# Attention products with V issued four items after a unit's scores instead of three

## Chip, cores and metric

The kernel runs on one core of one Trainium2 chip. The metric is the device time of one execution in microseconds (us). Engines are named as the profile names them: PE is TensorE's matmul stream and PEld its weight loads, DVE is VectorE, ACT is ScalarE, POOL is GpSimd, SP is SyncE, which issues the DMAs here.

## What is computed

Chunked attention with memory keys, then two feed-forward layers. In short:

```python
# attention: batch 4, heads 8, sequence 768, head size 64, chunks of 32 queries
for c in range(24):
    k_full = concat([mem_k, k[l_start:r_end]])      # 8 memory rows and up to 56 rows around the chunk
    a = softmax(scale * q_c @ k_full.T)
    out[c] = a @ v_full
x = out.transpose(0, 2, 1, 3).reshape(3072, 512)
h = x @ w_in                                        # 512 -> 2048
x = np.maximum(0.01 * h, h) @ w_out                 # 2048 -> 512
return (x @ w_a) * (x @ w_b) @ w_out2               # 512 -> 1536 -> 512
```

## The kernel before

**Attention units.** The 3072 tokens are cut into 24 units of 128 tokens. Four units make one block of 512 tokens, the width of a matmul in the layers behind. For each unit six steps run: `a_scores` (L193, 32 small matmuls of q and k into the PSUM tile `s`), `a_soft1` (L212, on DVE the maximum L215 and the subtraction L217, on ACT the exponential L220), `a_soft2` (L223, sum, reciprocal and scaling on DVE, L230 to L233), `a_turn` (L237, sixteen 32x32 DVE transposes L246 into the tile `pt`), `a_pv` (L266, 32 small matmuls L276 of `pt` and `v` into the PSUM tile `pv`), and `a_out` (L286), which splits `pv` into a rounded part `xh` by an ACT copy (L289) and a remainder `xl` by a DVE subtraction (L290). `xh` and `xl` of a block are what the first layer reads. `load_v` (L437) issues the two V loads (L189) of the unit after next on SP; their buffers are those that `a_pv` has just read.

**First layer.** The loop over `items` (L590) runs the first feed-forward layer block by block. Block 0 has 19 items and block 1 to 5 have 16 each; an item is one slice `f` of 128 hidden features. In an item `mm1` (L377) multiplies x with a slice of w_in: 12 matmuls (L303 reads `xh`, L304 reads `xl`, L305 reads `xh`). ACT and DVE make the activation `g` from the PSUM tile `h` (L383, L385) and split it into `gh` and `gl` (L320, L321; L321 runs on POOL in block 0, on DVE later). `mm2` (L388) multiplies the `g` of the item two before with w_out: 12 matmuls (L400, L403, L404) into the four PSUM tiles `a` of the block. After a block's last `mm2` ACT and DVE copy these four tiles out (L414, L412); the next block's `mm2` writes the same four tiles. In block 0 the two halves of 256 tokens run shifted by three items, so that its items have two 256-wide parts.

**What stands beside the items.** The dictionary `beside` (L428) lists for an item the attention steps of the next block's units; they are issued right after the item's `mm1` and `mm2` (L609). For a unit whose scores stand at item f, the steps stood at f (scores, loads of q and k, first softmax part), f+1 (second part), f+2 (transposes), f+3 (products with V, V loads, copies to x). The next unit's scores stand at f+3 as well, behind those products. In block 0 the scores stand at items 5, 8, 11, 14, in blocks 1 to 4 at 2, 5, 8, 11.

**Weights.** In block 0 the first layer's weights are made from raw 64-bit words: DVE joins them (L83, L86, L87), ACT rounds (L93), POOL subtracts (L94). In blocks 1 to 4 `prep_steps` (L476) does the same for the third and fourth layer's weights, in a ring of raw load (L473), ACT scaling (L79), DVE joins and sums (L83 to L87, L490 to L493), ACT rounding, POOL subtraction and a store (L507, L517), with one buffer for each stage. The weights of `mm2` come back from memory by the loads `w<-wod` (L586).

**What sets the order.** Each engine runs its own instructions in the order in which they stand in its queue. The queues are not written out by hand: a scheduler makes them when the kernel is built, from the program order and from when it reckons an operand to be ready, so that on DVE, ACT and SP steps of neighbouring items are mixed. On PE the order is that of the program except where operands were reckoned late.

Of the kernel before, what the change touches and what calls it, by code (L numbers as in the profile page):

```python
# [18 lines left out]
UT = 128  # L19
# [5 lines left out]
NF1, NF2 = F1 // P, F2 // P  # L25
# [6 lines left out]
def kernel(  # L32
# [30 lines left out]
    ps_h, ps_s, ps_a = [p.__enter__() for p in psum1]  # L63
# [353 lines left out]
    HALF, LEAD = TB // 2, 3  # L417
# [12 lines left out]
    def at(bi, f, fn, *args):  # L430
        beside.setdefault((bi, f), []).append(lambda: fn(*args))
# [19 lines left out]
    at(0, 1, a_out, 3, ("x", 0), 3 * UT)  # L451
    at(0, 1, load_v, 3)
    at(0, 1, load_qk, 3)
    for bi in range(NB3 - 1):
        for k, f in enumerate([5, 8, 11, 14] if bi == 0 else [2, 5, 8, 11]):
            u = (bi + 1) * (TB // UT) + k
            at(bi, f, a_scores, u)
            at(bi, f, load_qk, u)
            at(bi, f, a_soft1, u)
            at(bi, f + 1, a_soft2, u)  # L460
            at(bi, f + 2, a_turn, u)
            at(bi, f + 3, a_pv, u, ps_s, "s")
            at(bi, f + 3, load_v, u)
            at(bi, f + 3, a_out, u, ("x", bi + 1), k * UT)

# [277 lines left out]
    later = []  # L745
# [87 lines left out]
```

## Time and profile before

| | us |
|---|---|
| median of 3 runs | 1226.71 (1224.39 to 1227.79) |
| the profiled execution | 1226.21 |
| its span in the trace | 1224.4 |
| PE busy | 1170.7 |
| DVE busy | 752.9 |
| ACT busy | 383.1 |
| POOL busy | 145.4 |

The profile has a page with the busy time of each engine, and the trace behind it can be asked for the waits of an engine, for a timeline of its instructions and for busy times by stage. In a timeline a row gives start, duration, engine, line, operation, output and inputs, and in square brackets the idle time of the engine before the instruction with the instruction that ended it. A waiting matmul shows the idle time of PE, not of the whole kernel.

### The profile page before, as it was taken

The numbers are of one execution on the slowest core, as the hardware profiler recorded it, in microseconds if no ns is written. First come the engines' busy times: TensorE is split into PE (matmuls) and PEld (weight loads), VectorE is DVE, ScalarE is ACT, GpSimd is POOL, SyncE is SP. The second block draws the span as 40 slices with busy tenths as digits, with TensorE's granted clock in tenths as the row PEclk, the third lists the DMA queues.
The fourth block names the chain that finished last, engine by engine and source line by source line (L and its number), as shares of the span: only waits on it lengthen the run. The fifth ranks groups of instructions, "written<-read, shape, count | busy, mean of one in ns | idle before, by whom it ended". The sixth has DMA issues, their size and how long they took to land.

```text
span 1224.4 us, 16825 instructions
## 1 busy us (share of the span) xinstructions
PE 1170.7 (96%) x6632; PEld 984.1 (80%) x6632; DVE 752.9 (61%) x1313; ACT 383.1 (31%) x642; POOL 145.4 (12%) x109
## 2 busy tenths in 40 slices
PE   5788799989998999999999999999999999999998
PEld 5778788867887887888888888888888888888887
DVE  5999959795897899666622443447443447433443
ACT  3634333243334433222422222224122223222220
POOL 1544512032122222000000000000000000000000
PEclk9898999989999999999999999999999999999999
DMA  9766658768887887642633843537453535453512
GB/s 322 256 229 194 210 186 306 268 238 299 297 304 254 310 311 261 212 138 86 221 106 108 319 158 120 193 125 280 162 215 130 198 131 208 158 204 120 189 61 103
DMA packets 63822, 250.72 MB, mean 205 GB/s; under 512 B 7424, under 2 KB 8832, under 8 KB 56832
## 3 DMA queue, kind: packets, MB, share of 16 engines
q1 hardware_dynamic: 63744, 249.66, 57.5%
q8 instruction: 52, 0.85, 0.3%
q14 instruction: 26, 0.21, 0.1%
HBM read 200.34 MB, written 49.28 MB: 204 GB/s over the span
## 4 chain that ended last, share of the span: by engine, by line
PE 67%; DVE 2%; DMA 1%; issue 0%; POOL 0%; SPq 0%; DVEq 0%; POOLq 0%
PE o L729 5%; PE o L730 5%; PE o L731 5%; PE A L662 4%; PE A L663 4%; PE A L664 4%; PE h L303 4%; PE a L403 4%; PE a L404 4%; PE a L400 4%; PE h L304 3%; PE h L305 3%; PE C L662 3%; PE C L663 3%; PE C L664 3%; PE D L663 1%
## 5 line engine op out<-in xcount | busy, mean ns | idle before, releaser
L303 PE MATMUL h<-xh,w 128*128 128x512 f32 (+1 forms) x448 | 168.8, 377 | 17.5 <-POOL w L94 14.7
L400 PE MATMUL a<-gh,w 128*128 128x512 f32 (+1 forms) x448 | 161.3, 360 | 4.8 <-DVE x L412 2.3
L304 PE MATMUL h<-xl,w 128*128 128x512 f32 (+1 forms) x448 | 164.2, 367 | 0.5 <-DVE xl L290 0.5
L305 PE MATMUL h<-xh,w 128*128 128x512 f32 (+1 forms) x448 | 163.7, 365 | 0.0
L403 PE MATMUL a<-gl,w 128*128 128x512 f32 (+1 forms) x448 | 160.8, 359 | 0.0
L404 PE MATMUL a<-gh,w 128*128 128x512 f32 (+1 forms) x448 | 160.8, 359 | 0.0
L303 PEld LDWEIGHTS h<-xh,w 128*128 128x128 f32 x448 | 87.5, 195 | 33.2 <-POOL w L94 15.7
L729 PE MATMUL o<-w,cl 128*128 128x512 f32 x288 | 112.1, 389 | 0.2 <-DMA w<-wod 0.2
L730 PE MATMUL o<-w,ch 128*128 128x512 f32 x288 | 112.0, 389 | 0.0
L731 PE MATMUL o<-w,ch 128*128 128x512 f32 x288 | 112.0, 389 | 0.0
L385 DVE TENSOR_TENSOR g<-t,h 128x512 f32<-128x512 f32 (+1 forms) x99 | 66.1, 668 | 67.3 <-ACT t L383 66.5
L320 ACT CAST gh<-g 128x512 fp32r<-128x512 f32 (+1 forms) x99 | 60.1, 607 | 149.5 <-DVE g L385 144.1
L246 DVE STREAM_TRANSPOSE pt<-p 32x128 f32<-32x128 f32 x320 | 96.8, 302 | 5.5
L400 PEld LDWEIGHTS a<-gh,w 128*128 128x128 f32 x448 | 84.6, 189 | 18.6 <-DVE x L412 2.9
L304 PEld LDWEIGHTS h<-xl,w 128*128 128x128 f32 x448 | 87.7, 196 | 13.1 <-DVE xl L290 0.9
L305 PEld LDWEIGHTS h<-xh,w 128*128 128x128 f32 x448 | 87.0, 194 | 13.3
L404 PEld LDWEIGHTS a<-gh,w 128*128 128x128 f32 x448 | 84.7, 189 | 12.5
L403 PEld LDWEIGHTS a<-gl,w 128*128 128x128 f32 x448 | 84.6, 189 | 12.5
L383 ACT ACTIVATE t<-h 128x512 f32<-128x512 f32 (+1 forms) x99 | 57.5, 581 | 110.3 <-PE h L305 110.3
L684 DVE TENSOR_TENSOR ga<-u,C 128x512 f32<-128x512 f32 x36 | 24.8, 688 | 105.4 <-ACT u L676 76.2
L676 ACT COPY u<-A 128x512 f32<-128x512 f32 x72 | 42.3, 587 | 143.5 <-PE A L664 143.5
L662 PE MATMUL A<-ch,wab 128*128 128x512 f32 x216 | 84.1, 389 | 0.0
(95 smaller groups left out, 2116.3 us busy)
## 6 DMA issues: line engine op xcount, KB each, us to landing
wab<-wab SPq DMA_DIRECT2D x36, 1792.0 KB, 7.3
w<-wod SPq DMA_DIRECT2D x116, 512.0 KB, 4.7
raw<-w SPq DMA_DIRECT2D x68, 512.0 KB, 5.9
wab<-pw SPq DMA_DIRECT2D x12, 1792.0 KB, 6.7
k<-kl SPq DMA_DIRECT2D x48, 256.0 KB, 4.3
v<-vl SPq DMA_DIRECT2D x48, 256.0 KB, 4.7
wod<-w SPq DMA_DIRECT2D x16, 512.0 KB, 5.3
q<-ql SPq DMA_DIRECT2D x48, 128.0 KB, 4.1
```

Source lines behind the costliest of these rows:

```text
L246: nc.vector.transpose(out=pt[o0:o0 + 32, :, 2 * cpar + hpar, hpx, :], in_=p[i0:i0 + 32, hpx::2, 32 * b:32 * b + 32],)
L303: nc.tensor.matmul(ps, w[1], x[0], start=first, stop=False)
L304: nc.tensor.matmul(ps, w[0], x[1], start=False, stop=False)
L305: nc.tensor.matmul(ps, w[0], x[0], start=False, stop=last)
L400: nc.tensor.matmul(ps, slot[:, 1, c], gh[:, t], start=f == 0 and o == 0, stop=False, **kw)
L403: nc.tensor.matmul(ps, slot[:, 0, c], gl[:, t], start=False, stop=False, **kw)
L404: nc.tensor.matmul(ps, slot[:, 0, c], gh[:, t], start=False, stop=f == NF1 - 1, **kw)
L662: nc.tensor.matmul(ps, w[:, 1, i, c], hi[:, kc], start=first and kc == 0, stop=False, **kw)
L663: nc.tensor.matmul(ps, w[:, 0, i, c], lo[:, kc], start=False, stop=False, **kw)
L729: nc.tensor.matmul(o, cl[:, q], w[:, 0, :], start=k == 0, stop=False)
L730: nc.tensor.matmul(o, ch[:, q], w[:, 1, :], start=False, stop=False)
L731: nc.tensor.matmul(o, ch[:, q], w[:, 0, :], start=False, stop=k == NCH - 1)
```

## The change

For the units of blocks 1 to 5 (u = 4 to 23) the three steps `a_pv`, `load_v` and `a_out` are put at f+4 instead of f+3, if that item still exists in the block; otherwise they stay at f+3. With scores at 5, 8, 11, 14 of 19 items, and at 2, 5, 8, 11 of 16 items, f+4 is at most 18 and at most 15, so that all 20 units move.

```diff
+    def last_item(bi):
+        return NF1 + LEAD if bi == 0 else NF1
+
     for bi in range(NB3 - 1):
         for k, f in enumerate([5, 8, 11, 14] if bi == 0 else [2, 5, 8, 11]):
             u = (bi + 1) * (TB // UT) + k
             at(bi, f, a_scores, u)
             at(bi, f, load_qk, u)
             at(bi, f, a_soft1, u)
             at(bi, f + 1, a_soft2, u)
             at(bi, f + 2, a_turn, u)
-            at(bi, f + 3, a_pv, u, ps_s, "s")
-            at(bi, f + 3, load_v, u)
-            at(bi, f + 3, a_out, u, ("x", bi + 1), k * UT)
+            later = (bi, f + 4) if f + 4 < last_item(bi) else (bi, f + 3)
+            at(*later, a_pv, u, ps_s, "s")
+            at(*later, load_v, u)
+            at(*later, a_out, u, ("x", bi + 1), k * UT)
```

## Rows read from the trace of the kernel before

**Rows 1.** The page's first part: busy time, share of the span and instructions of each engine.

```profile
PE 1170.7 (96%) x6632; PEld 984.1 (80%) x6632; DVE 752.9 (61%) x1313; ACT 383.1 (31%) x642; POOL 145.4 (12%) x109
```

**Rows 2.** The waits of PE: who waited for whom, total us, how many times, the longest.

```profile
PE pv L276 <- DVE pt L246: 18.5, 16, 2.7
PE h L303 <- POOL w L94: 14.7, 6, 5.8
```

**Rows 3.** Busy time by stretch: the second half of block 0, the end of block 1, and most of block 3. Columns: stretch, its length, busy us (instructions) of PE, PEld, DVE, ACT and POOL, granted clock, DMA share, GB/s.

```profile
84.00:168.00 84.00, 68.43 (x637) 65.42 (x636) 73.92 (x136) 32.77 (x60) 36.39 (x27) 0.88 0.57 188
244.00:278.00 34.00, 29.07 (x169) 23.52 (x165) 30.77 (x59) 14.12 (x25) 10.00 (x6) 0.90 0.69 251
388.00:470.00 82.00, 82.00 (x537) 68.32 (x536) 70.34 (x143) 33.59 (x56) 18.10 (x13) 1.00 0.87 302
```

**Rows 4.** Timeline of PE: the first matmul of `mm1` in items of blocks 3 to 5 that run without a stall. The first pair has a V product and scores between its items, the second pair scores alone, the third a V product alone; the item after the last pair has neither.

```profile
537.49 0.39 PE L303 MATMUL h<-xh,w 128*128 128x512 f32 x1
...
551.48 0.39 PE L303 MATMUL h<-xh,w 128*128 128x512 f32 x1
...
499.59 0.39 PE L303 MATMUL h<-xh,w 128*128 128x512 f32 x1
...
512.63 0.39 PE L303 MATMUL h<-xh,w 128*128 128x512 f32 x1
...
576.35 0.39 PE L303 MATMUL h<-xh,w 128*128 128x512 f32 x1
...
588.53 0.39 PE L303 MATMUL h<-xh,w 128*128 128x512 f32 x1
...
593.97 0.39 PE L303 MATMUL h<-xh,w 128*128 128x512 f32 x1
```

**Rows 5.** Timelines of PE and DVE in block 0: `mm1` of item 14, the copy of unit 6 to x and the first softmax step of unit 7 on DVE, and the `mm2` of block 0 that waits for a copy out of its PSUM tiles.

```profile
132.61 0.35 PE L303 MATMUL h<-xh,w 128*128 128x256 f32 x1 [1.19 <-DVE g L385]
...
151.50 0.69 DVE L290 TENSOR_TENSOR xl<-pv,xh 128x512 fp32r<-128x512 f32 x1 [1.75 <-ACT xh L289]
152.11 0.68 DVE L215 TENSOR_REDUCE m<-s 128x8 f32<-128x512 f32 x1
...
163.12 0.39 PE L400 MATMUL a<-gh,w 128*128 128x256 f32 x1 [1.97 <-ACT x L414]
```

**Rows 6.** Timelines of PE, ACT and DVE at the end of block 1 and the start of block 2: `mm1` of item 14, the longest stop inside a V product (unit 11), the first `mm1` of block 2, and the stop of its first `mm2`.

```profile
257.73 0.50 PE L303 MATMUL h<-xh,w 128*128 128x512 f32 x1 [0.66 <-DVE g L385]
...
267.52 0.47 PE L276 MATMUL pv<-pt,v 128*64 128x64 f32 x2 [2.71 <-DVE pt L246]
...
277.50 0.39 PE L303 MATMUL h<-xh,w 128*128 128x512 f32 x1
...
293.79 0.65 ACT L79 ACTIVATE raw<-raw 128x512 f32<-128x512 f32 x1 [1.71 <-DMA raw<-w]
...
294.47 0.43 DVE L83 TENSOR_SCALAR pz<-raw 128x512 int32<-128x512 int32 x1 [2.49 <-ACT raw L79]
294.82 0.69 DVE L412 COPY x<-a 128x512 f32<-128x512 f32 x1
...
295.56 0.50 PE L400 MATMUL a<-gh,w 128*128 128x512 f32 x1 [2.25 <-DVE x L412]
```

**Rows 7.** The same at the end of block 2 and the start of block 3 (unit 15).

```profile
368.85 0.39 PE L303 MATMUL h<-xh,w 128*128 128x512 f32 x1
...
377.25 0.33 PE L276 MATMUL pv<-pt,v 128*64 128x64 f32 x2 [2.53 <-DVE pt L246]
...
386.63 0.39 PE L303 MATMUL h<-xh,w 128*128 128x512 f32 x1
...
400.73 0.43 DVE L83 TENSOR_SCALAR pz<-raw 128x512 int32<-128x512 int32 x1 [2.42 <-ACT raw L79]
401.07 0.69 DVE L412 COPY x<-a 128x512 f32<-128x512 f32 x1
```

**Rows 8.** Timelines of SP, DVE and PE at the end of block 3: the store of a prepared weight, the DVE work behind it, the copy of unit 19 to x, and the first `mm1` of block 4.

```profile
469.44 0.38 SPq L507 DMA_DIRECT2D wab<-pw  x1
...
484.02 2.67 DVE L83 TENSOR_SCALAR pz<-raw 128x512 int32<-128x512 int32 x1 [0.63 <-POOL pw L94]
...
488.06 0.68 DVE L290 TENSOR_TENSOR xl<-pv,xh 128x512 fp32r<-128x512 f32 x1
488.80 0.50 PE L304 MATMUL h<-xl,w 128*128 128x512 f32 x1 [0.51 <-DVE xl L290]
```

**Rows 9.** Timelines of PE, ACT and DVE near the end of block 4: the V product of unit 23 and its copies to x.

```profile
581.88 1.15 PE L276 MATMUL pv<-pt,v 128*64 128x64 f32 x32
583.08 0.59 ACT L289 CAST xh<-pv 128x512 fp32r<-128x512 f32 x1 [1.78 <-PE pv L276]
583.70 0.69 DVE L290 TENSOR_TENSOR xl<-pv,xh 128x512 fp32r<-128x512 f32 x1 [1.67 <-ACT xh L289]
```

**Rows 10.** Timeline of PE between block 0 and block 1: the first `mm1` of block 1 (512 columns) and an `mm2` of block 0 (256 columns) that runs between its matmuls.

```profile
169.81 0.40 PE L303 MATMUL h<-xh,w 128*128 128x512 f32 x1
...
171.87 0.28 PE L400 MATMUL a<-gh,w 128*128 128x256 f32 x1
```

**Rows 11.** The waits of SP's queue for the V loads (total us, times, longest), and the page's row of V loads (instructions, KB of each, us from issue to landing).

```profile
SPq L189 <- PE pv L276: 18.2, 14, 4.4
...
v<-vl SPq DMA_DIRECT2D x48, 256.0 KB, 4.7
```

## The prediction

> **What bounds the kernel now.** I read the page's first part, then the waits of PE, then the busy times by stretch, and last the timelines at the places that the change touches. PE is busy for 1170.7 of 1224.4 us [rows 1], so time can only come from the 54 us in which it stands. The largest item of these is the one that the change is about: V products that wait for the DVE transposes of `pt`, 18.5 us in 16 waits [rows 2]. The question is whether PE would get past the place where it now waits, or only stand a little further on. The stretches answer part of it. In the second half of block 0, DVE is busy for 73.9 of 84 us and PE for 68.4; at the end of block 1, DVE for 30.8 of 34 us and PE for 29.1; in most of block 3, PE is busy all of 82 us [rows 3]. So there are two regimes. Where V products wait, DVE is the busier engine and is behind PE; elsewhere PE sets the pace. The change takes no work from DVE: the same transposes, softmax steps and copies run. It only lets PE do an item's first-layer matmuls before it asks for `pt`.
>
> **What the V waits cost as they stand.** An undisturbed item lasts 588.53 to 593.97, 5.44 us. Two items with a V product between them take 576.35 to 588.53, 12.18 us [rows 4]. Around unit 11, at the end of block 1, the same two items take 257.73 to 277.50, 19.77 us, so 7.6 us are lost there [rows 6], more than the waits themselves, because the granted clock falls as well (0.90 over the stretch [rows 3]). Around unit 15, at the end of block 2, they take 368.85 to 386.63, 17.78 us: 5.6 us lost [rows 7]. These two are the large places of blocks 1 to 4. With 7.6 and 5.6 us the most that the change can win there is 13.2 us, and block 0's share comes on top.
>
> **Part 1, block 0 (units 4 to 7).** PE would not wait at items 8, 11 and 14, but DVE still runs behind. At item 14 `mm1` already waits for `g`, on DVE, until 132.61 [rows 5]: what PE wins before that point it gives back there, as DVE's queue does not depend on it. What does get through is in the order on DVE: now the copy of unit 6, L290 at 151.50, for which DVE itself stands 1.75 us, is ahead of L215 of unit 7 at 152.11. With the copy an item later, L215 can start 1.75 + 0.61 = 2.36 us earlier (0.61 is the distance of the two starts), and with it the softmax, the transposes and the copy out of PSUM that releases `mm2` at 163.12 [rows 5]. I take 1.3 us of these 2.36, since part of what follows waits for weight preparation instead; bounds are 0 and 4.3 (2.36 and the whole stop of 1.97 at 163.12).
>
> **Part 2, end of block 1.** Here up to 7.6 us could be won [rows 6], and I take nothing. Block 2's first `mm2` waits until 295.56 for the PSUM copy L412 of 294.82, which is queued on DVE behind L83 of 294.47, which waits for ACT's L79 of 293.79, which waits for a raw weight load [rows 6]. That is the preparation ring, one buffer to a stage, which goes back to DVE work that is behind anyway. If PE comes earlier, its stop there grows from 2.25 us by what it has won. Bounds: 0, if the queue stays as it is, and -7.6 us if it is ordered otherwise.
>
> **Part 3, end of block 2.** Lost now: 5.6 us [rows 7]. The next stop is of the same kind, L412 at 401.07 behind L83 of 400.73 [rows 7], but PE does not wait for it today, so there is some room. I take 1.5 us, with bounds of 0 and 5.6.
>
> **Part 4, end of block 3.** The first `mm1` of block 4 waits for `xl` until 488.80, and `xl` waits in DVE's queue until 488.06 behind L83, which ran from 484.02, held by POOL [rows 8]. The chain goes back to the store of 469.44 on SP, which PE's own progress releases, so earlier gains pass through, but PE cannot start block 4's `mm1` before DVE comes to `xl`. What PE can win is `mm2` work done ahead while it waits, up to five matmuls of 5.44 / 24 = 0.227 us: I take 0.5 us, bounds 0 and 1.1.
>
> **Part 5, the price of parting V products and scores.** Today the V products of unit u and the scores of unit u+1 stand in one item, back to back. Two items with both between them take 537.49 to 551.48, 13.99 us: 3.11 over 10.88 (two plain items). Scores alone: 499.59 to 512.63, 13.04, so 2.16. V products alone: 12.18, so 1.30 [rows 4]. Parted they cost 3.46 instead of 3.11, 0.35 us for each pair, since PE changes between large and small matmuls twice as often. There are three pairs in each block, 15 in all: 5.2 us, if PE paces everywhere. In blocks 0 to 2 the stops of parts 1 to 3 absorb it, which leaves the 6 pairs of blocks 3 and 4: +2.1 us, bounds 0 and 5.2.
>
> **Part 6, block ends.** The last unit's products now stand in the last item, directly ahead of the next block's `mm1`, which reads their copies. Undisturbed, the chain runs from 583.03 (581.88 + 1.15) over the ACT copy at 583.08 and the DVE subtraction at 583.70 to 584.39: 1.36 us [rows 9]. Today an item lies between and hides it. What can cover it is the `mm2` of the item two before, which needs nothing of x: twelve matmuls, half an item, 2.7 us. That the queue is made in this way is seen once: between blocks 0 and 1 an `mm2` of the old block runs at 171.87 amid the new block's `mm1` that began at 169.81 [rows 10]. I take +0.2 us in all, bounds 0 and 4 x 1.36 = 5.4.
>
> **The loads.** Two V loads for each unit wait on SP for the V products, 18.2 us in 14 waits, and land 4.7 us after issue [rows 11]. They fetch for the unit after next, six items or some 33 us before use, so one item less leaves 27. They hold up what stands behind them on SP, weight loads and raw loads; since PE reaches them no later in the places with long waits, I take nothing. If SP's queue kept its order and each wait grew by an item, it would slow the ring of part 2; bounds 0 and +2.6 (a mean wait, 18.2 / 14 = 1.3 us, at the ends of blocks 1 and 2). The PSUM buffers of the small products alternate as before, as scores and products still take turns.
>
> **The sum.** -1.3 - 0 - 1.5 - 0.5 + 2.1 + 0.2 = -1.0 us against the profiled execution's 1226.21 (its span is 1224.4), so 1225.2. The median of the runs, 1226.71, lies 0.5 above it: 1225.7 by that. I say **1225.3**, practically no change.
>
> **Rivals.** (a) *The gains pass.* If queues on DVE come out so that the copies L412 are not behind the ring, all of PE's gains count: -1.3 (block 0), -4.9 (block 1: 7.6 less the chain of part 6, taken twice because DVE is behind there: 7.6 - 2.7), -4.2 (block 2: 5.6 - 1.4), -0.5, and all 15 pairs cost +5.2: -5.7 us, 1221.0. With L412's 2.25 us gone too, 1218.7. For it: DVE is idle before L83 for 2.49 and 2.42 us [rows 6, 7], so the copies could go first. Against it: nothing in the change moves them. (b) *Block ends become the stop.* If the new block's `mm1` is queued right behind the V products, PE stands for the chain `pv`, `xh`, `xl` at the ends of blocks 2, 3 and 4, where no other stop absorbs it: 1.36 us at best and with DVE behind as at 484 to 488 some 2 us more [rows 8, 9], say 3 each, +9 over part 6's 0.2, while the gains of parts 1 to 4 stay: 1225.3 + 8 = about 1233; with 1.36 each, 1229.2. It decides from the point where the chain is longer than the `mm2` work queued ahead. The trace shows PE standing at 295.56 for one operand while other matmuls of the next items had theirs: it does not look past the head of its queue [rows 6]. [...] (c) *The change does nothing at all*, because the queue already places late V products elsewhere: against it, all V products in blocks 1 to 4 that I followed stand at f+3, and its time would be 1226.7, inside the forecast's case.
>
> **Chances.** No change, by the sum: 0.47 (with (c)). Rival (a): 0.34. Rival (b): 0.19. A measurement of this kernel can tell about 0.3%, 3.7 us, from no change, that is 1223.0 to 1230.4. The forecast's own range is 1222 to 1229. With the bounds of the parts, the range that should hold 8 in 10 goes from 1217.5 (rival (a) with L412's wait gone and a little more in block 0) to 1231.5 (rival (b) at two block ends).
>
> **What would show it.** Right: the V products' wait for `pt` falls from 18.5 us to under 3; PE's waits for `xl` and `g`, for weights by POOL, or for L412 grow by most of it; the first `mm2` of block 2 still starts after a wait near 295; an item with V products alone takes 1.30 us more and one with scores alone 2.16. The forecast is wrong if PE's waits in blocks 0 to 4 together fall by over 8 us (then (a)), or if waits of L303 or L304 for `xh` and `xl` come up to over 5 us (then (b)).

## The result and the profile after

The changed kernel takes 1242.2 us (median of 4 runs, 1240.13 to 1243.06) against 1226.52 for the kernel before in the same measurement: a ratio of 1.0127, 95% interval [1.0108, 1.0146], so 15.7 us slower. The forecast was 1225.3, its range ended at 1231.5. Its profiled execution has a span of 1240.3 us, 15.9 more than that of before.

Lines behind the change stand 4 lower in the changed kernel: the ring's stores L507 and L517 are L511 and L521 there. Its page begins, span and busy times:

```profile
span 1240.3 us, 16791 instructions
...
PE 1177.6 (95%) x6632; PEld 983.2 (79%) x6632; DVE 756.1 (61%) x1313; ACT 382.4 (31%) x642; POOL 145.8 (12%) x109
```

The waits of PE in the changed kernel (total us, times, longest):

```profile
...
PE h L303 <- ACT xh L289: 10.7, 3, 4.2
PE a L400 <- ACT gh L320: 7.7, 3, 3.5
...
PE h L303 <- DVE g L385: 5.7, 4, 2.4
...
PE a L400 <- DVE x L412: 1.2, 1, 1.2
```

The change did what it says: the 18.5 us of V products waiting for `pt` [rows 2] are gone, not a row is left. In their place stand three waits of the first layer for `xh`, 10.7 us, and three of `mm2` for `gh`, 7.7 us. They lie at the ends of blocks 1, 2 and 3, one pair at each. The worst is the end of block 3. Timelines of SP, PE, ACT, DVE and POOL there:

```profile
491.41 2.37 POOL L94 TENSOR_TENSOR pw<-ps,pw 128x1024 fp32r<-128x1024 f32 x1 [1.45 <-ACT pw L93]
491.52 2.81 DVE L87 SCALAR_TENSOR_TENSOR pz<-raw,pz 128x512 int32<-128x512 int32 x1
492.14 1.15 PE L276 MATMUL pv<-pt,v 128*64 128x64 f32 x32
493.81 0.32 SPq L511 DMA_DIRECT2D wab<-pw  x1
494.25 0.68 DVE L385 TENSOR_TENSOR g<-t,h 128x512 f32<-128x512 f32 x1
494.96 0.62 ACT L320 CAST gh<-g 128x512 fp32r<-128x512 f32 x1 [3.14 <-DVE g L385]
495.63 0.50 PE L400 MATMUL a<-gh,w 128*128 128x512 f32 x1 [2.34 <-ACT gh L320]
...
497.58 0.69 DVE L321 TENSOR_TENSOR gl<-g,gh 128x512 fp32r<-128x512 f32 x1 [0.69 <-ACT gh L320]
500.57 0.62 ACT L93 CAST pw<-pz 128x512 fp32r<-128x512 f32 x1 [3.02 <-DMA wab<-pw]
501.09 0.58 ACT L289 CAST xh<-pv 128x512 fp32r<-128x512 f32 x1
501.72 0.79 PE L303 MATMUL h<-xh,w 128*128 128x512 f32 x1 [4.19 <-ACT xh L289]
502.31 0.63 PE L403 MATMUL a<-gl,w 128*128 128x512 f32 x1
...
503.63 0.68 DVE L290 TENSOR_TENSOR xl<-pv,xh 128x512 fp32r<-128x512 f32 x1
504.37 0.79 PE L304 MATMUL h<-xl,w 128*128 128x512 f32 x1 [0.58 <-DVE xl L290]
```

Read it from the bottom up. PE stands 4.19 us at 501.72 for `xh`. The V products that `xh` copies ended at 493.29 (492.14 + 1.15), and the copy takes 0.58 us, yet it runs only at 501.09. The row ahead of it in ACT's queue says why: the weight ring's rounding L93 stood for the store `wab<-pw`, because the ring has one buffer `pw` and the store still reads it. The store was issued at 493.81, so ACT was held until 6.8 us later. Nothing of attention waits for that weight; `xh` merely stands behind it. The earlier stop, 2.34 us at 495.63, is DVE's: L87 of the ring took 2.81 us beside POOL's L94, and `g`, `gh` and then `mm2` came late. PE stands in order as well: the `mm2` matmuls queued behind the waiting `mm1` had their operands (the later `gl` was ready at 498.27), but ran only from 502.31. Behind this stop the granted clock is low. Busy time by stretch in the changed kernel, columns as in [rows 3]:

```profile
501.70:507.40 5.70, 5.10 (x12) 3.56 (x13) 2.32 (x4) 0.00 (x0) 0.83 (x1) 0.52 0.59 234
507.50:520.00 12.50, 12.50 (x57) 10.32 (x56) 5.22 (x8) 5.34 (x9) 1.29 (x1) 1.00 0.62 210
```

In the first stretch the granted clock is 0.52, and matmuls back to back start 0.43 us apart (505.39, 505.82, 506.25); in the second it is 1.00, and they start 0.23 us apart (508.31, 508.54, 508.77). Over the 5.7 us the lost clock is worth an estimated 2.7 us (5.7 x 0.48). At the end of block 1 the same picture, PE and ACT of the changed kernel:

```profile
270.54 1.15 PE L276 MATMUL pv<-pt,v 128*64 128x64 f32 x32
...
280.17 0.62 ACT L93 CAST pw<-pz 128x512 fp32r<-128x512 f32 x1 [2.56 <-DMA wab<-pw]
280.69 0.58 ACT L289 CAST xh<-pv 128x512 fp32r<-128x512 f32 x1
...
281.33 0.80 PE L303 MATMUL h<-xh,w 128*128 128x512 f32 x1 [3.29 <-ACT xh L289]
```

ACT of the kernel before, same place:

```profile
272.65 0.56 ACT L289 CAST xh<-pv 128x512 fp32r<-128x512 f32 x1
...
279.54 0.62 ACT L93 CAST pw<-pz 128x512 fp32r<-128x512 f32 x1 [2.54 <-DMA wab<-pw]
```

The rounding waited there too, just as long, but `xh` was ahead of it. The end of block 2 in the changed kernel, PE and ACT, has the order of the other two:

```profile
383.30 1.15 PE L276 MATMUL pv<-pt,v 128*64 128x64 f32 x32
...
390.12 0.62 ACT L93 CAST pw<-pz 128x512 fp32r<-128x512 f32 x1 [1.91 <-DMA wab<-pw]
390.64 0.58 ACT L289 CAST xh<-pv 128x512 fp32r<-128x512 f32 x1
```

At the end of block 4 the ring has ended, and there the step works as forecast. Timelines of PE, ACT and DVE in the changed kernel, which answer to [rows 9]:

```profile
603.68 1.15 PE L276 MATMUL pv<-pt,v 128*64 128x64 f32 x32
604.76 0.50 PE L400 MATMUL a<-gh,w 128*128 128x512 f32 x1
604.88 0.59 ACT L289 CAST xh<-pv 128x512 fp32r<-128x512 f32 x1 [1.78 <-PE pv L276]
605.50 0.69 DVE L290 TENSOR_TENSOR xl<-pv,xh 128x512 fp32r<-128x512 f32 x1 [1.67 <-ACT xh L289]
...
605.79 0.40 PE L303 MATMUL h<-xh,w 128*128 128x512 f32 x1
```

`mm2` matmuls fill the time until the copies are there, and no instruction of PE waits.

**The account.** The start of an item's first `mm1` matmul is a landmark that both kernels have. The table gives how much later it is than before (minus: earlier), and what each stretch adds, worked out from the timelines of PE; the last two columns are the version with two tiles of the experiments below.

| stretch, up to the start of | before, us | changed: difference | added | two tiles: difference | added |
|---|---|---|---|---|---|
| block 0 and block 1, item 13 of block 1 | 251.47 | -2.52 | -2.52 | -3.20 | -3.20 |
| end of block 1, item 4 of block 2 | 305.13 | +2.42 | +4.94 | -7.30 | -4.10 |
| block 2, its item 14 | 368.85 | +3.48 | +1.06 | -6.24 | +1.06 |
| end of block 2, item 3 of block 3 | 404.97 | +5.46 | +1.98 | -10.01 | -3.77 |
| block 3, its item 14 | 474.26 | +6.52 | +1.06 | -8.94 | +1.07 |
| end of block 3, item 3 of block 4 | 507.06 | +15.30 | +8.78 | -6.23 | +2.71 |
| block 4, its item 14 | 576.35 | +16.36 | +1.06 | -5.16 | +1.07 |
| end of block 4, item 3 of block 5 | 604.85 | +16.37 | +0.01 | -5.16 | 0.00 |

Block ends 1 to 3 cost 15.7 us, the parted pairs 3.2, and block 0 with most of block 1 gives 2.5. Some 0.5 us come back later, to the span's 15.9. Of the 15.7 us, 11.0 are time in which PE stands (23.3 us at the three block ends, 12.3 before). The other 4.7 are a longer busy time for about as many matmuls, at a granted clock of 0.88, 0.91 and 0.88 where it was 0.90, 0.95 and 1.00.

Each column is one trace, and small terms are not safe in it. In experiments 5, 7 and 10 below, which move no V product of block 0, block 1 begins 2.1 to 2.6 us earlier than before as well. So the -2.5 can't be put down to the change by this table; the 15.7 can.

### The profile page after: what moved, and what is told of

It is laid out like the page before. It is cut to its first block, busy times and chain, and to the rows that moved or that the text cites. A ratio compares the mean times of both kernels' runs of the same rounds, so it can differ in the third digit from the quotient of the medians.

```text
span 1240.3 us, 16791 instructions
## 1 busy us (share of the span) xinstructions
PE 1177.6 (95%) x6632; PEld 983.2 (79%) x6632; DVE 756.1 (61%) x1313; ACT 382.4 (31%) x642; POOL 145.8 (12%) x109
## 4 chain that ended last, share of the span: by engine, by line
PE 59%; DMA 1%; DVE 0%; POOL 0%; ACT 0%; issue 0%; DVEq 0%; ACTq 0%
PE o L734 5%; PE o L733 5%; PE o L735 5%; PE A L667 4%; PE A L666 4%; PE A L668 4%; PE C L666 3%; PE C L667 3%; PE C L668 3%; PE h L303 2%; PE a L400 2%; PE a L404 2%; PE a L403 2%; PE h L304 2%; PE h L305 2%; PE D L667 1%
## 5 line engine op out<-in xcount | busy, mean ns | idle before, releaser
L303 PE MATMUL h<-xh,w 128*128 128x512 f32 (+1 forms) x448 | 172.2, 384 | 32.7 <-POOL w L94 15.4
L400 PE MATMUL a<-gh,w 128*128 128x512 f32 (+1 forms) x448 | 163.9, 366 | 15.1 <-ACT gh L320 7.7
L304 PE MATMUL h<-xl,w 128*128 128x512 f32 (+1 forms) x448 | 166.9, 373 | 0.8 <-DVE xl L290 0.8
L305 PE MATMUL h<-xh,w 128*128 128x512 f32 (+1 forms) x448 | 166.0, 371 | 0.0
L404 PE MATMUL a<-gh,w 128*128 128x512 f32 (+1 forms) x448 | 161.9, 361 | 0.0
L303 PEld LDWEIGHTS h<-xh,w 128*128 128x128 f32 x448 | 88.9, 199 | 51.4 <-POOL w L94 16.4
L385 DVE TENSOR_TENSOR g<-t,h 128x512 f32<-128x512 f32 (+1 forms) x99 | 66.1, 667 | 80.1 <-ACT t L383 79.4
L305 PEld LDWEIGHTS h<-xh,w 128*128 128x128 f32 x448 | 89.2, 199 | 13.3
L246 DVE STREAM_TRANSPOSE pt<-p 32x128 f32<-32x128 f32 x320 | 96.8, 302 | 4.5
L667 PE MATMUL A<-cl,wab 128*128 128x512 f32 x216 | 84.1, 389 | 0.0
```

Source lines behind the costliest of these rows:

```text
L246: nc.vector.transpose(out=pt[o0:o0 + 32, :, 2 * cpar + hpar, hpx, :], in_=p[i0:i0 + 32, hpx::2, 32 * b:32 * b + 32],)
L303: nc.tensor.matmul(ps, w[1], x[0], start=first, stop=False)
L304: nc.tensor.matmul(ps, w[0], x[1], start=False, stop=False)
L305: nc.tensor.matmul(ps, w[0], x[0], start=False, stop=last)
L400: nc.tensor.matmul(ps, slot[:, 1, c], gh[:, t], start=f == 0 and o == 0, stop=False, **kw)
L404: nc.tensor.matmul(ps, slot[:, 0, c], gh[:, t], start=False, stop=f == NF1 - 1, **kw)
```

## Experiments

The theory after the result: block ends are the loss, because `xh` of the last unit stands behind the ring's rounding in ACT's queue. The rivals: the loss comes from parting the products in general, or DVE is too late anyway and ACT only seems to be the cause, or the V loads hold up SP. Each experiment is an edit of the changed kernel unless it says otherwise, each ratio is against the kernel before on the same chip.

**1. All but the last unit of blocks 1 to 4 moved.**

```diff
-            later = (bi, f + 4) if f + 4 < last_item(bi) else (bi, f + 3)
+            later = (bi, f + 4) if bi == 0 or k < 3 else (bi, f + 3)
```

> Units of block 0's items and the first three units of each later block moved to f+4, the last unit of blocks 1 to 4 left at f+3. Theory Q (the ACT copy xh of a block's last unit is queued behind the weight ring's ACT rounding L93, which waits for a store; the next block's first mm1 waits for xh): the waits of L303 for xh, 10.7 us, go to 0, the V products of units 11, 15 and 19 wait for pt again; the 12 parted pairs of blocks 1 to 4 cost 4.2 us and block 0 gives 2.5: 1228 us (1226 to 1231). Rival S (parting V products and scores is the cost): nearly all of the loss stays, 1239 to 1242. Rival L (later V loads hold SP and the ring): three quarters stay, 1238.

Measured 1234.71 us, 1.0068 [1.0046, 1.0090]: a miss by 6.7 us. Leaving the last unit where it was removes half the loss. At the end of block 3 PE still stands for `xh`; timelines of POOL, DVE, ACT and PE of this version:

```profile
490.27 2.39 POOL L94 TENSOR_TENSOR pw<-ps,pw 128x1024 fp32r<-128x1024 f32 x1 [1.78 <-ACT pw L93]
490.39 2.83 DVE L87 SCALAR_TENSOR_TENSOR pz<-raw,pz 128x512 int32<-128x512 int32 x1
...
493.85 0.62 ACT L320 CAST gh<-g 128x512 fp32r<-128x512 f32 x1 [3.16 <-DVE g L385]
494.37 0.58 ACT L289 CAST xh<-pv 128x512 fp32r<-128x512 f32 x1
...
495.00 0.80 PE L303 MATMUL h<-xh,w 128*128 128x512 f32 x1 [2.46 <-ACT xh L289]
```

Here `xh` stands behind `gh`, which waits for DVE, which is held in the ring's L87 beside POOL. No store is in it. So ACT's wait for the store is not the only way in which the ring gets ahead of `xh`.

**2. Only the last unit moved.**

```diff
-            later = (bi, f + 4) if f + 4 < last_item(bi) else (bi, f + 3)
+            later = (bi, f + 4) if bi > 0 and k == 3 else (bi, f + 3)
```

> Only the last unit of blocks 1 to 4 moved to f+4, all others at f+3. Theory Q: the loss at the ends of blocks 1 to 3 stays, 14 us by the landmarks of the two traces, without parted pairs: 1240 us (1237 to 1243). Rival S: no pair is parted, 1226 to 1228. Rival L: one unit in five, 1229.

Measured 1234.72 us, 1.0070 [1.0051, 1.0090]: a miss by 5.3 us. Half of the loss again, with 11.3 us of waits for `xh` in 3 places. Experiments 1 and 2 together give 1.4%, the whole change 1.27%: within the intervals the two halves add up.

**3. Block 0 alone.**

```diff
-            later = (bi, f + 4) if f + 4 < last_item(bi) else (bi, f + 3)
+            later = (bi, f + 4) if bi == 0 else (bi, f + 3)
```

> Only the four units in block 0's items moved. Block 1's item 2 came 2.5 us earlier in the changed kernel, but the stops at 257.73 and 295.56 of the kernel before may take it back. If it passes: 1224. If it is taken back by the ring: 1226.5. Rival S: three more parted pairs, 1227.5.

Measured 1223.81 us, 0.9985 [0.9971, 1.0000]. The interval allows a gain from nothing to some 3.5 us. In the trace block 5 begins 2.55 us earlier than before, but on the way the lead was 3.26, 2.02, 4.09 and 3.68 us (blocks 1, 1, 2 and 3), so it is not plainly one gain that is carried through. Against experiment 1 it follows that units 0 to 2 of blocks 1 to 4 cost 10.9 us (1234.71 - 1223.81), of which parting, the first rival, explains at most 12 x 0.35 = 4.2.

**4. The ring's rounding on POOL** instead of ACT, so that no wait for the store stands in ACT's queue; the ring's four calls pass `nc.gpsimd` as `rnd`.

```diff
-        nc.scalar.copy(hi, z)
+        if rnd is None:
+            nc.scalar.copy(hi, z)
+        else:
+            rnd.tensor_copy(hi, z)
```

> The full change, and the ring's rounding (L93 pw) moved from ACT to POOL in front of POOL's subtraction, so that nothing that waits for the ring's store stands in ACT's queue. Theory Q: the waits of L303 for xh fall from 10.7 to under 2 us and of L400 for gh from 7.7 to under 4; with less cold clock some 12 us come back: 1230 (1226 to 1234). Rival D (DVE is behind at the block ends and xh would be late anyway): the waits change their name, 1238 to 1243. POOL's own price is unknown; if POOL and DVE hold each other up more, up to 5 us on either number.

Measured 1230.44 us, 1.0030 [1.0017, 1.0043]. The waits for `xh` fall from 10.7 to 2.4 us, those for `gh` from 7.7 to 3.1. Those for `xl`, on DVE, rise from 0.8 to 5.7: in part the wait moves on to the next engine.

**5. The same edit on the kernel before**, to see what the edit costs by itself.

> The kernel before, with the ring's rounding on POOL instead of ACT: the control for the run that did the same to the changed kernel (1230.4). Theory Q (the change loses because block ends come to depend on ACT and DVE queues that the weight ring holds): the ring's rounding costs the kernel before little, 1220 to 1227, so that the change still costs some 3 to 8 us with POOL rounding instead of 16. If the rounding on POOL simply helps any kernel by 12 us: 1213, and the ACT queue has no special part in the change's loss.

Measured 1230.07 us, 1.0040 [1.0026, 1.0053]: a miss, the edit costs about 4 us of its own. Under it the change makes no difference (1230.44 against 1230.07, measured beside different runs of before: 1.0030 to 1.0040). With the ring's rounding out of ACT's queue, the 15.7 us that the change cost are gone.

**6. `pw` as two tiles**, each stored when it is ready, so that the rounding of the next weight needs only the smaller, earlier store to be through.

```diff
-                w = prep.tile([P, 2, 7, 256], F32R, tag="pw", name="pw", bufs=1)
+                wa = prep.tile([P, 2, 3, 256], F32R, tag="pw", name="pw", bufs=1)
+                wb = prep.tile([P, 2, 4, 256], F32R, tag="pwb", name="pwb", bufs=1)
...
+                nc.sync.dma_start(out=wabd[p, m][:, :, 0:3, :], in_=wa.bitcast(F32))
...
-                nc.sync.dma_start(out=wabd[p, m], in_=w.bitcast(F32))
+                nc.sync.dma_start(out=wabd[p, m][:, :, 3:7, :], in_=wb.bitcast(F32))
```

> The full change, with the ring's buffer pw cut into two tiles (3 and 4 of the 7 forms), each stored as soon as it is done, so that the next rounding L93 on ACT waits for the first, earlier store only. Theory Q: ACT's waits of L93 pw for the store fall, xh comes some 2 to 3 us earlier at each of three block ends: 1234 to 1238. Rival D (DVE's lag decides, the store's wait only stands where DVE's would): 1240 to 1243.

Measured 1222.61 us, 0.9974 [0.9958, 0.9990]: better than expected by over 11 us, and faster than both kernels. Its waits, of PE:

```profile
PE h L303 <- ACT xh L289: 1.9, 3, 1.2
```

ACT's wait for the store, in this version, in the changed kernel and in the kernel before:

```profile
ACT pw L93 <- DMA wab<-pw: 3.4, 3, 2.2
```

```profile
ACT pw L93 <- DMA wab<-pw: 9.3, 4, 3.0
```

```profile
ACT pw L93 <- DMA wab<-pw: 7.2, 4, 2.5
```

At the end of block 3, timelines of DVE, PE and ACT of the version with two tiles:

```profile
476.06 2.87 DVE L87 SCALAR_TENSOR_TENSOR pz<-raw,pz 128x512 int32<-128x512 int32 x1
477.79 1.15 PE L276 MATMUL pv<-pt,v 128*64 128x64 f32 x32
479.56 0.62 ACT L320 CAST gh<-g 128x512 fp32r<-128x512 f32 x1 [3.16 <-DVE g L385]
480.09 0.62 ACT L93 CAST pw<-pz 128x512 fp32r<-128x512 f32 x1
...
481.95 0.62 ACT L320 CAST gh<-g 128x512 fp32r<-128x512 f32 x1 [0.75 <-DVE g L385]
482.47 0.58 ACT L289 CAST xh<-pv 128x512 fp32r<-128x512 f32 x1
483.11 0.50 PE L303 MATMUL h<-xh,w 128*128 128x512 f32 x1 [1.18 <-ACT xh L289]
```

L93 is still ahead of `xh` but does not wait; `xh` starts 3.5 us after the V products' end (478.94), where it was 7.8 in the changed kernel. DVE is held as long as there (L87 2.87 us, 2.81 in the changed kernel), and `gh` waits as long for it (3.16 and 3.14). So with DVE's delay left as it was, this block end adds 2.7 us in the table instead of 8.8.

**7. Two tiles on the kernel before.**

> The kernel before with the ring's buffer in two tiles: the control for the run that did so to the changed kernel (1222.6). Theory Q: in the kernel before no PE wait hangs on ACT's L93, so two tiles give it little, 1224 to 1227, and the change is then worth 2 to 4 us where the ring does not hold ACT. If the two tiles simply speed up every kernel by 15 to 20 us: 1207 to 1211.

Measured 1225.59 us, 1.0011 [1.0000, 1.0021]. Two tiles alone give nothing. So the change is worth 0.9974 / 1.0011 = 0.9963 with two tiles, about -4.5 us, and +15.7 us without them. The loss is an interaction of the move with the one buffer, not a price of the move alone.

**8. `xh` of the last unit on DVE** (blocks 1 to 4), which takes it out of ACT's queue.

```diff
-        nc.scalar.copy(hi[:, :, off:off + UT], o)
+        if off == 3 * UT and u >= 8:
+            nc.vector.tensor_copy(hi[:, :, off:off + UT], o)
+        else:
+            nc.scalar.copy(hi[:, :, off:off + UT], o)
```

> The full change, with the rounding copy xh of the last unit of blocks 1 to 4 on DVE instead of ACT. Theory Q: the stop behind L93 on ACT goes; DVE's own queue at the block ends is some 2 to 4 us behind: L303 waits for xh 3 to 6 us in all instead of 10.7, 1234 to 1238. Rival D: DVE is as late as ACT, 1241 to 1245.

Measured 1238.46 us, 1.0099 [1.0079, 1.0120], just outside the expected range: a gain of some 3 us on the changed kernel's 1.0127, and the two intervals overlap. PE now waits 8.4 us for `xh` on DVE (3 times, longest 5.7). DVE carries the ring's joins and is nearly as late as ACT: the second rival holds in part.

**9. Only the copies moved** (`a_out` at f+4, the products and loads at f+3).

```diff
-            at(*later, a_pv, u, ps_s, "s")
-            at(*later, load_v, u)
+            at(bi, f + 3, a_pv, u, ps_s, "s")
+            at(bi, f + 3, load_v, u)
             at(*later, a_out, u, ("x", bi + 1), k * UT)
```

> Only the copies to x at f+4; V products and V loads stay at f+3. Theory Q: what hurts is where the copy of the last unit stands in ACT's and DVE's queues, not where PE has the products: V products wait for pt as before (18 us) and L303 waits for xh at the block ends on top, since PE has nothing of x until the last item: 1235 to 1241, no parted pairs. Rival P (PE's own order, products directly ahead of mm1, is the cost): 1225 to 1228.

Measured 1229.96 us, 1.0033 [1.0020, 1.0046]: a miss. The V products wait 18.9 us, as before (18.5), and PE never waits for `xh`: it reaches the block ends too late for that. So it takes an early PE as well for the waits for `xh`. The late copy still costs 4 us: PE's waits for L412 grow from 2.3 to 5.1 us, and by the landmarks 2.3 us are lost at the end of block 2, where 2.1 us of them lie, and 2.1 us in block 1. Why is open.

**10. Only the V loads moved.**

```diff
-            at(*later, a_pv, u, ps_s, "s")
+            at(bi, f + 3, a_pv, u, ps_s, "s")
             at(*later, load_v, u)
-            at(*later, a_out, u, ("x", bi + 1), k * UT)
+            at(bi, f + 3, a_out, u, ("x", bi + 1), k * UT)
```

> Only the V loads at f+4; products and copies stay at f+3. Theory Q: no effect, 1225 to 1228. Rival L (later V loads hold SP's queue and with it the ring): a good part of the 16 us, over 1230.

Measured 1222.79 us, 0.9992 [0.9979, 1.0004]: no effect. Here the V loads stand less on SP for V products than before (13.8 us against 18.2), so this run alone does not test the third rival. In the changed kernel they stand 22.6 us, and with two tiles, where the loss is gone, 20.8. By both the rival falls.

**11. Block 0 alone, with two tiles.**

> Only block 0's units moved, with the two tiles. If the two add up: 2.5 us under the kernel before with two tiles; by theory Q 1222 to 1224. It beats the full change with two tiles (1222.6) only if the 12 parted pairs of later blocks (4.2 us) cost more than the V waits they remove.

Measured 1221.57 us, 0.9982 [0.9967, 0.9998]. This can't be told from experiment 6 (0.9974): by these medians block 0 gives most of what the whole change gives with two tiles.

**12. All but the last unit, with two tiles.**

> All units moved but the last of blocks 1 to 4, with the two tiles. Theory Q: the loss of the one-tile form of this (1234.7) was the ring as well, so 1221 to 1226. If that loss came from the parted pairs or from the V waits that stay, it keeps 1231 to 1235.

Measured 1226.44 us, 1.0022 [1.0010, 1.0034]. Two tiles take 0.46% off experiment 1, though no wait for the store stood directly ahead of `xh` at the stop shown there: the ring's position against PE changes as well. It is still 0.48% above experiment 6, which moves one unit more in each block. In the traces the two part at the end of block 3, which adds 7.3 us here and 2.7 there. Here PE waits 2.5 us for `pt` again, and 1.9 us at 496.49 for the copy L414; ACT runs that copy at 495.86, behind the ring's L79, which had waited 6.35 us for a raw weight load until 492.13, and behind the ring's L93. So the ring holds ACT's queue here too, by another DMA. Its share in the 0.48% was not tested.

## Why the prediction was wrong

**What was right.** The V products no longer wait (18.5 us to 0, forecast under 3). The price of parting is 0.35 us for each pair: three pairs add 1.06 us in the middle of each of blocks 2 to 4 here and in experiments 1, 4, 6, 8 and 12, and experiment 2, which parts none of them, adds 0.00 there. In the changed kernel, PE's `mm1` starts near the end of block 4, the first gap with scores, the second with a V product, the last two with neither:

```profile
572.93 0.39 PE L303 MATMUL h<-xh,w 128*128 128x512 f32 x1
...
580.39 0.50 PE L303 MATMUL h<-xh,w 128*128 128x512 f32 x1
...
587.14 0.50 PE L303 MATMUL h<-xh,w 128*128 128x512 f32 x1
...
592.71 0.39 PE L303 MATMUL h<-xh,w 128*128 128x512 f32 x1
...
598.15 0.39 PE L303 MATMUL h<-xh,w 128*128 128x512 f32 x1
```

From 572.93 to 592.71 are 19.78 us, 3.46 over three plain items, as part 5 had worked it out [rows 4]. At block 4's end the `mm2` fill of part 6 holds, and the V loads cost nothing.

**Term by term, the sum against the table.**

- Part 1, block 0: forecast -1.3, measured -2.5. DVE's order changed as forecast: L215 runs at 148.79, ahead of L290 at 158.78, and the copy L412 comes 2.29 us earlier (160.96 against 163.25), close to the uncut 2.36 [rows 5]. That this is what the end gains is not shown: other traces have as large a lead without it, and experiment 3 allows 0 to 3.5 us.
- Part 5: forecast +2.1, measured +3.2. Block 2 pays its 1.06 as well; in blocks 0 and 1 it does not show.
- Parts 2, 3, 4 and 6, the ends of blocks 1 to 3: forecast -1.5 - 0.5 + 0.2 = -1.8, measured +15.7. This is the step that failed. The clock, which the prediction noted for the V waits but did not price here, adds to it: 0.52 behind the stop at block 3. So time does not come only from PE's standing, as the prediction's first paragraph has it: the busy time of the same 6632 matmuls rose from 1170.7 to 1177.6 us.

**What failed in it.** Part 6 priced the chain `pv`, `xh`, `xl` at 1.36 us from block 4 [rows 9], the one block end where the ring had ended. There it is 1.36 again, and hidden. At the other three ends the time from the V products to `xh` was 9.0, 6.2 and 7.8 us (280.69 - 271.69, 390.64 - 384.45, 501.09 - 493.29), since `xh` stood in ACT's queue behind `gh`, held by DVE, and behind L93, held by a store. Half an item of `mm2`, 2.7 us, covers little of that. Rows of block 3 [rows 8] showed DVE behind the ring; the prediction did not weigh what stands ahead of `xh` in ACT's queue, though ACT's wait for `wab<-pw` stood in the trace of before (7.2 us in 4 waits).

**The rivals.** Rival (b) named what happened, block ends become the stop, with the `pv`, `xh`, `xl` chain as its price: 1.36 to 3 us for each end. Measured were 4.9, 2.0 and 8.8, at the ends of blocks 1, 2 and 3; it had named 2, 3 and 4, and block 4's end cost nothing. Its engine was wrong too: it looked at DVE and `xl`, where PE stood for ACT and `xh` (`xl` cost 0.8 us). Rival (a), the gains pass, is what the version with two tiles shows: -4.1 and -3.8 us at the ends of blocks 1 and 2 against -4.9 and -4.2, and 1222.6 us against 1221.0. That the numbers are so near is in part luck: with two tiles on the kernel before, block 1's end alone comes 6.7 us forward without the move, and block 2's end 1.6 us back. Part 2's stop at L412, which was to take the gain back, stayed small. Two rows of PE in the changed kernel, items in block 1 and block 2:

```profile
257.08 0.50 PE L303 MATMUL h<-xh,w 128*128 128x512 f32 x1 [2.40 <-DVE g L385]
...
299.15 0.50 PE L400 MATMUL a<-gh,w 128*128 128x512 f32 x1 [1.16 <-DVE x L412]
```

Before, these waits were 0.66 and 2.25 us [rows 6]. The first did take back block 1's gain for an item, as part 2 expected of DVE; the second shrank, when PE came 2.4 us later (305.13 in the table).

**What stays open.** That the loss hangs on the ring's rounding in ACT's queue and on its one buffer is shown twice, each time with a control: by experiments 4 with 5 and 6 with 7. That ACT's wait for the store is the whole of the way is not shown. At the three block ends L93 waits 2.56, 1.91 and 3.02 us, 7.5 together, and two tiles take off more than that. Both edits also move other steps of the ring: over the three block ends POOL is busy for 23 us with two tiles and 32 in the changed kernel. At the end of block 3, where DVE's hold is the same in experiment 6, 2.7 us of 8.8 remain; at the other ends the shares are not known, experiment 1 has stops by DVE alone, and experiment 8 moves the stop to DVE. Why the scheduler puts L93 ahead of `xh` when the product moves by an item was not tried. The remainders of experiments 9 and 12, 4 and 6 us, are placed but have no tested cause.

## What to carry to other kernels

When a step is moved, list for each engine that its results pass what is queued there and what *that* waits for: at the end of block 3 the rounding L93 stood 3.02 us until the ring's own store had freed a single buffer, and `xh`, which has nothing to do with that store, ran behind it at 501.09, 7.8 us after its products. Price a chain at every place where it will run, not at the one place where it is undisturbed. And an early arrival is worth only as much as the next late operand lets through: here cutting one background buffer in two turned +15.7 us into a small gain.

## What was not expected of the hardware

Joins of the ring on DVE that started early in one of POOL's 128x1024 subtractions L94 lasted until POOL was done. In the changed kernel six of them, which started 0.07 to 0.41 us after L94, took 2.58 to 2.81 us and ended 0.28 to 0.55 us after it; the median of L83 is 0.43 us, that of L86 and of L87 0.69. At 491.52 L87 took 2.81 us and ended at 494.33, 0.55 us after POOL (493.78); in experiment 1 it took 2.83 us, ending 0.56 after POOL. Nearby in the changed kernel, at 504.24, the same instruction took 0.68 us with no L94 beside it, and the transposes L246 that ran beside such an L94 at 329.13 took 0.30 us each, no longer than elsewhere. Why these joins are held and those transposes are not was not tested. The hold at 491.52 lies in the middle of the path to `g`, which L385 makes from 494.25 on.

The other surprise is how far landmarks move and come back. With two tiles on the kernel before, block 2's item 5 starts 7.2 us earlier than in the kernel before, and block 5 only 0.84: here a gain in the middle of the kernel said little about its end.
